# SiLU from ScalarE in every chunk, the second product of the first two chunks as a block, and a new plan of work

## The chip, the cores and the metric

The kernel runs on one core of a Trainium2 chip. The core has a matrix engine (TensorE, "PE" in the profile, with its weight loads as "PEld"), VectorE ("DVE"), ScalarE ("ACT"), GpSimd ("POOL") and SyncE ("SP"), each with a queue of its own that it works through in order. Data are loaded and stored by DMA; a DMA is issued from the queue of an engine. The metric is the time of one execution on the device in microseconds (us). Eleven runs of the kernel before have a median of 275.7 us (272.99 to 277.82).

## The reference

Linear attention, then a SiLU feed-forward layer, over 8 batches of 8 heads, 576 positions and 64 features a head (4608 tokens of 512 features, hidden width 2048):

```python
q_s = exp(q - max(q, -1));  q_s = q_s / (sum(q_s, -1) + 1e-09)      # over features
k_s = exp(k - max(k, 2));   k_s = k_s / (sum(k_s, 2) + 1e-09)       # over positions
kv = einsum('bhsd,bhse->bhde', k_s, v)
x = einsum('bhsd,bhde->bhse', q_s, kv)       # then tokens x (heads * features)
h = x @ w_in                                 # 512 -> 2048
g = h * (1.0 / (1.0 + np.exp(-h)))
out = g @ w_out                              # 2048 -> 512
```

Inputs and output are float32; the kernel multiplies in bf16 and leaves the maxima out, which cancel.

## The kernel before

**Tiling.** The attention works by batch (576 tokens), the feed-forward layer by chunk of 512 tokens, nine of them (chunk 0 takes 576 tokens in its first product, chunk 1 the 448 that are left of 1024). For a batch, `exp` makes eq and ek on ScalarE, two instructions each (`cc` is the half of the heads); `qsum` sums eq on VectorE, `qnorm` divides by the sum, `tr_dma` transposes eq by a DMA into qT; `vcast` writes v in bf16 beside a column of ones into vaug; `kv` multiplies ek by vaug (36 matmuls of 64x65 for each half), so that the last column holds k's sum, and `kvcopy` divides by it. `xt` then makes x transposed in PSUM, `xtcopy` casts it to the tile XT. There is one tile each of eq, ek, vaug and of the loaded q, k and v, so the next batch's exponentials wait until the tile before has been read.

**The first product** is h transposed: W1 is the stationary operand, XT the moving one. In chunks 0 and 1 it is done directly (`mm1`, four matmuls for each 128 hidden features), and `act1` makes SiLU as tanh on ScalarE (tile sg) and `(tanh + 1) * h` on VectorE (line 259); the factor 0.5 comes at the end. From chunk 2 on a part is done by Strassen's scheme in Winograd's form (`product1`, line 316): seven products of half size in place of eight, for a group of 4 x 128 hidden features. The token columns are split in two, the features that are summed over in two, the hidden features in two. XT's sums and differences (`xsum`, tiles XS: S1 to S4) and W1's (`vsum`, tiles TX, once) are the operands; `sum1` (lines 333, 339, 341) combines the seven products in three PSUM banks to four results; `silu1` (line 355) applies ScalarE's SiLU. `std` in a chunk's plan says how many of the four groups are done directly: 2 in chunk 2, 1 in chunks 3 to 8.

**The second product** is direct in chunk 0 (`mm2`, line 476), and by the same scheme in chunks 1 to 8 (`product`, line 411: 14 units of 8 matmuls of 256 columns, seven products in two halves of the tokens). `presum` (lines 369 to 375) makes the sums of GT, the SiLU's output, in two halves of hidden features, into the tiles SW (S1, S2, S4) and in place; `wsum` makes W2's (tiles TW, once); `after` (lines 428 to 447) combines and `qstore` stores from SP. The second product of a chunk runs during the next chunk's first product.

**Order.** Nothing is scheduled by a tool: the order of every engine's queue is the order in which the program writes instructions. `PLAN[t]` gives each piece of work a position within chunk t, counted in units of the first product: `order` is the order of (group, product) pairs, `y` the positions of the 14 (or 16) units of the second product of the chunk before, `ex` of the next batch's four exponentials, `qs`/`qn` of sums and normalisation, `vs`/`ks`/`kc` of casts, kv products and their rescaling, `tp` of the transposing DMA, `ox`/`oc` of the attention product and its casts, `xs`/`xe` of the four XT sums and their engine (0 VectorE, 1 GpSimd), `pa`/`pae` and `pb`/`pbe` of the first and second half of the pre-sums and their engines, `add`, `act`, `ya` of combining steps. `put` gathers the pieces and they are written sorted by position. Chunks 3 to 7 share the plan STEADY. PSUM has eight banks: a ring of six for first products, attention and kv, and two for second products.

**Start.** Batch 0 is loaded from SP in halves. A tiny copy on GpSimd waits for the first half of v, and behind it GpSimd's queue issues the weights (float32 to bf16 on the way) and batch 1's q, k and v: W1 quarter 0, 1, W2 quarter 0, W1 2, W2 1, q, W1 3, k, W2 2, v, W2 3. `heat` keeps TensorE running on a zero tile meanwhile.

Of the kernel before, what the change touches and what calls it, by code (L numbers as in the profile page):

```python
# [15 lines left out]
PLAN = {  # L16
    0: {'y': [5.5, 6.5, 7.5, 8.5, 8.5, 9.5, 10.5, 11.5, 13.5, 13.8, 14.5, 15.5, 15.6, 15.7, 15.9, 22.5], 'ex': [8.9, 10.9, 12.9, 13.4], 'qs': [9.92, 11.4], 'qn': [10.43, 11.41], 'vs': [14.45, 15.05], 'ks': [15.65, 15.75], 'kc': [15.651, 15.751], 'lq': 14.06, 'tp': 12.9, 'ox': [16.35, 16.6], 'oc': [16.36, 18.61], 've': [2, 2]},
    1: {'ex': [0.9, 4.4, 5.9, 5.4], 'qs': [3.9, 4.9], 'qn': [4.91, 5.91], 'vs': [9.3, 10.9], 'ks': [12.4, 13.9], 'kc': [13.41, 14.91], 'lq': 10.45, 'lk': 12.4, 'lv': 15.41, 'tp': 11.4, 'ox': [16.4, 23.6], 'oc': [17.91, 23.61], 've': [1, 1], 'pa': [13.1, 17.7, 18.3], 'pae': [1, 0, 0]},
    2: {'std': 2, 'order': [(3, 1), (2, 1), (2, 6), (3, 6), (2, 2), (2, 7), (3, 2), (3, 7), (3, 5), (2, 5), (2, 4), (3, 3), (3, 4), (2, 3)], 'y': [-2.5, 1.5, 3.5, 4.5, 5.5, 7.5, 9.5, 11.5, 14.0, 15.5, 17.5, 19.0, 20.0, 21.0], 'ex': [-2.6, 0.41, 2.92, 0.43], 'qs': [2.9, 3.9], 'qn': [5.91, 5.91], 'vs': [3.42, 12.4], 'ks': [8.9, 16.4], 'kc': [10.91, 16.41], 'lq': -0.55, 'lk': -2.1, 'lv': 14.41, 'tp': 7.4, 'ox': [18.4, 19.4], 'oc': [18.91, 19.41], 'sl': [0.5, 1.5, 3, 3, 4.5, 8.5, 7, 7], 'add': {(3, 2): 17.02, (2, 7): 13.55, (3, 1): 10.02, (3, 6): 11.55, (2, 5): 17.55, (2, 3): 21.55, (3, 3): 19.55}, 'act': {(2, 6): 13.02, (2, 4): 19.02, (2, 3): 25.02, (2, 5): 17.55, (3, 2): 14.55, (3, 3): 23.02, (2, 1): 11.55, (3, 1): 9.55, (2, 7): 16.02}, 's1': {2: 0, 3: 0}, 'xs': [0.4, 0.9, 7.9, 4.4], 'pa': [16.45, 23.95, 19.45], 'ya': {3: 22.45, 6: 5.5, 5: 15.95, 2: 7.95}, 'm1': [1, 0], 'pb': [-0.4, 0.2, 2.1, 2.2, 2.8], 'xe': [0, 1, 1, 1], 'pae': [1, 1, 1], 'pbe': [0, 0, 0, 0, 0], 've': [1, 2]},
}  # L20
STEADY = {'std': 1, 'order': [(1, 1), (1, 6), (1, 2), (1, 7), (1, 5), (2, 1), (2, 6), (1, 4), (1, 3), (2, 2), (2, 7), (2, 5), (3, 1), (2, 4), (3, 6), (2, 3), (3, 7), (3, 2), (3, 5), (3, 4), (3, 3)], 'y': [1.5, 3.5, 5.5, 7.5, 9.5, 10.0, 15.5, 16.5, 17.5, 18.0, 22.0, 23.5, 24.2, 24.6], 'ex': [-5.1, -0.59, -4.08, -4.57], 'qs': [5.4, 6.4], 'qn': [5.91, 6.41], 'vs': [0.4, 7.42], 'ks': [11.9, 17.4], 'kc': [15.91, 17.41], 'lq': 9.95, 'lk': 16.9, 'lv': 9.41, 'tp': 8.9, 'ox': [22.4, 22.4], 'oc': [22.91, 23.41], 'sl': [2.0, 2.0, 6.5, 4.0], 'add': {(2, 2): 17.02, (1, 2): 6.55, (3, 2): 20.55, (3, 1): 16.55, (3, 7): 21.02, (1, 5): 9.55, (3, 5): 22.55}, 'act': {(1, 5): 12.02, (2, 6): 12.02, (1, 2): 7.02, (3, 1): 19.02, (1, 6): 9.02, (1, 1): 8.02, (3, 3): 25.55, (3, 5): 25.02, (1, 3): 14.02, (2, 2): 15.02, (2, 5): 16.55, (1, 4): 13.02, (3, 7): 23.02, (3, 6): 20.02}, 's1': {1: 1, 2: 0, 3: 0}, 'xs': [-1.6, 0.9, -1.6, 1.4], 'pa': [21.45, 21.95, 23.45], 'pb': [-0.05, 2.46, 2.95, -0.04, 2.95], 'ya': {4: 23.95, 5: 19.45}, 'm1': [0, 0], 'xe': [0, 0, 0, 0], 'pae': [1, 0, 0], 'pbe': [0, 0, 0, 0, 1], 've': [1, 1]}
for _t in range(3, 8):
    PLAN[_t] = STEADY
PLAN[8] = {'std': 1, 'order': [(1, 1), (1, 6), (1, 7), (1, 2), (1, 5), (2, 1), (2, 6), (1, 4), (1, 3), (2, 7), (3, 1), (2, 5), (2, 2), (3, 6), (2, 4), (2, 3), (3, 7), (3, 2), (3, 5), (3, 4), (3, 3)], 'y': [4.5, 5.0, 5.0, 7.5, 9.5, 10.5, 15.5, 17.5, 18.0, 19.0, 22.0, 23.7, 25.5, 26.6], 'sl': [4.0, 10.0, 7.5, 6.0], 'add': {(1, 2): 9.02, (3, 1): 16.02, (1, 5): 9.55}, 'act': {(2, 5): 18.02, (1, 3): 13.02, (1, 4): 15.02, (1, 6): 8.02, (2, 3): 22.02, (3, 3): 25.55, (3, 2): 24.02, (2, 1): 11.02, (3, 5): 22.55, (1, 5): 9.55, (3, 1): 15.55, (1, 2): 8.02, (1, 1): 5.02, (1, 7): 10.02, (2, 4): 19.02, (2, 2): 20.02, (2, 7): 16.02}, 's1': {1: 1, 2: 1, 3: 0}, 'xs': [-11.1, -0.1, 3.4, 7.9], 'pa': [19.95, 20.95, 22.95], 'pb': [-5.55, -4.04, 4.45, -0.04, 2.95], 'ya': {6: 9.5, 3: 27.05, 2: 10.95, 5: 20.95, 1: 7.0, 7: 18.95, 4: 25.7}, 'm1': [0, 0], 'xe': [0, 0, 0, 0], 'pae': [0, 0, 0], 'pbe': [0, 0, 0, 1, 0]}
PLAN[9] = {'y': [0, 1, 2, 3, 4, 5, 6, 7, 8, 9, 10, 11, 12, 13], 'ya': {}, 'm1': [0, 0], 'pb': [-0.5, -0.4, -0.3, 1.9, 2.9], 'pbe': [0, 0, 0, 0, 0]}
TXAT = [(0, (0, 11.76, 1, 0)), (1, (0, 15.77, 1, 0)), (2, (0, 14.78, 1, 1)), (3, (0, 15.79, 1, 1)), (0, (2, 3.1, 0, 0)), (1, (2, 5.6, 0, 0)), (2, (2, 5.6, 0, 0)), (3, (2, 9.6, 0, 1))]
TWAT = [(0, 10.1, 1), (0, 8.7, 1), (0, 13.0, 1), (0, 13.6, 1), (0, 14.7, 0), (0, 19.3, 1), (0, 17.9, 1), (0, 14.0, 1)]

@with_exitstack
def kernel(  # L30
# [26 lines left out]
    part = [[(0, 5 * P), (5 * P, S - 5 * P)]] + [[(0, cut[t + 1] - cut[t])] for t in range(1, NCH)]  # L57
# [34 lines left out]
    def load(b, name, src, ccs=None, eng=nc.sync):  # L92
        if name not in st[b]:
            st[b][name] = ld.tile([128, NG, J * D], FP32, name=name, bufs=LDB[name])
        x = src[b].rearrange("(g r) (p j) d -> g (r p) (j d)", r=2, j=J).rearrange("g x y -> x g y")
        c = slice(0, NG) if ccs is None else slice(2 * ccs, 2 * ccs + 2)
        eng.dma_start(out=st[b][name][:, c, :], in_=x[:, c, :])
# [4 lines left out]
    def exp(b, src, dst, cc):  # L102
        if dst not in st[b]:
            st[b][dst] = ap.tile([128, J, NG * D], BF16, name=dst, bufs=1)
        o = st[b][dst][:, :, cc * 128:(cc + 1) * 128].rearrange("p j (g d) -> p j g d", d=D)
        nc.scalar.activation(out=o, in_=jgd(st[b][src], cc), func=ACT.Exp)  # L106

    def vcast(b, cc, eng):
        o = vaug.rearrange("p j (g e) -> p j g e", e=E1)[:, :, 2 * cc:2 * cc + 2, 0:D]
        if eng is nc.scalar:  # L110
            eng.copy(out=o, in_=jgd(st[b]["vt"], cc))
        else:
            eng.tensor_copy(o, jgd(st[b]["vt"], cc))

    def qsum(b, cc):
# [3 lines left out]
        e = st[b]["eq"][:, :, cc * 128:(cc + 1) * 128].rearrange("p j (g d) -> p j g d", d=D)  # L119
        nc.vector.reduce_sum(out=st[b]["zq"][:, cc], in_=e, axis=AX.X)  # L120
# [15 lines left out]
    def tr_dma(b, eng):  # L136
# [3 lines left out]
        )  # L140

    TG = 6

    def tr(b, g):
        t = ps.tile([128, TG, 128], BF16, name="qtps", tag="ring", bufs=PSB["ring"])
        st[b]["qtps", g] = t
# [541 lines left out]
```

The softmax here doesn't subtract the row's maximum and nothing guards it: scores larger than these inputs give would overflow.

## Time and profile before

The table is from one profiled execution, which took 275.42 us on the device and whose span from the first to the last instruction is 273.6 us.

| | before |
|---|---|
| median of 11 runs | 275.7 us (272.99 to 277.82) |
| profiled execution, its own time | 275.42 us |
| its span | 273.6 us |
| busy: PE / VectorE / ScalarE / GpSimd | 256.9 / 210.6 / 172.7 / 110.9 us |
| mean granted TensorE clock | 0.994 |
| first product of chunk 0 begins | 16.6 us |
| first product of chunk 1 begins | 49.0 us |
| first product of chunk 2 begins | 72.3 us |
| first product of chunk 3 begins | 99.5 us |
| last matmul instructions begin as a block of 128 | 254.8 us |
| ACT_TABLE_LOAD | 12 |

A stage's line in the profile has the stretch (start and end in us from the span's start), its length, and then for PE, PE's weight loads, VectorE, ScalarE and GpSimd the busy time with the number of instructions in brackets, the mean granted TensorE clock, the share of the DMA engines' time that was busy, and GB/s. A line of the timeline has the start, the time, the engine, the source line, the operation, output and inputs, the number of instructions put together, and in square brackets how long the engine had been idle and what ended that. A line of the chain has the start, the time, and the engine with its work. Matmul ends are modelled, so the distance from one matmul to the next says more than the length of one.

### The profile page before, as it was taken

The page shows a single profiled execution, that of the slowest core. Times are in us where ns is not written, and L with a number is a line of the kernel's source. Part 1 is how long each engine was busy: PE and PEld are TensorE (multiplying, and loading weights), DVE is VectorE, ACT ScalarE, POOL GpSimd, SP SyncE. Part 2 cuts the span into 40 slices and gives each one's busy share as a digit, 9 for nine tenths or more (in the row PEclk, how much of TensorE's full clock was granted, in tenths as well). Part 3 has the DMA queues.
Part 4 walks back from the last instruction along what each step waited for, and adds up shares of the span by engine and source line. Part 5 has one row for each costly group of instructions (what it writes and reads, how often), then busy time and mean ns, then how long its engine had stood idle before and what let it go on. Part 6 is the DMA issues. An engine that isn't in the chain of part 4 may idle for free.

```text
span 273.6 us, 6402 instructions
## 1 busy us (share of the span) xinstructions
PE 256.9 (94%) x2594; PEld 191.7 (70%) x2594; DVE 210.6 (77%) x405; ACT 172.7 (63%) x276; POOL 110.9 (41%) x71
## 2 busy tenths in 40 slices
PE   8789989975899999999999999999999999999992
PEld 3356655432467768886888688868886887788882
DVE  2967487498399888889888988888887668877932
ACT  5665576794796499738964896498654457344400
POOL 1561678996159754650644064416332013100000
PEclk9999999999799999999999999999999999999999
DMA  7999999979919850499059805971613012201324
GB/s 257 294 190 244 328 302 215 384 243 217 345 16 366 200 164 20 79 311 363 13 95 361 291 18 99 368 267 30 126 42 78 2 38 58 60 10 32 89 66 115
DMA packets 42925, 46.48 MB, mean 170 GB/s; under 512 B 18576, under 2 KB 30864, under 8 KB 42896
## 3 DMA queue, kind: packets, MB, share of 16 engines
q1 hardware_dynamic: 37856, 38.35, 47.7%
q0 software_dynamic: 5040, 7.73, 12.8%
q8 instruction: 20, 0.33, 0.5%
q14 instruction: 9, 0.07, 0.1%
HBM read 36.70 MB, written 9.44 MB: 169 GB/s over the span
## 4 chain that ended last, share of the span: by engine, by line
PE 69%; DMA 14%; DVE 5%; issue 5%; POOL 4%; ACT 1%; POOLq 0%; ACTq 0%
PE ops L411 34%; PE hps L316 22%; PE hps L233 9%; DMA W<-in_moe_w_out_dram 8%; DMA qT<-eq 3%; DMA qt<-in_q_dram 3%; PE o L203 2%; POOL eq L126 1%; PE kvps L168 1%; DVE TX L291 1%; ACT sg L247 1%; POOL W L516 1%; PE ops L476 1%; DVE zq L120 1%; DVE SW L375 1%
## 5 line engine op out<-in xcount | busy, mean ns | idle before, releaser
L233 PE MATMUL hps<-XT,W 128*128 128x512 bf16 (+3 forms) x320 | 61.3, 337 | 1.9 <-DVE GT L259 1.7
L411 PEld LDWEIGHTS <-GT 128*128 128x128 bf16 x512 | 50.3, 98 | 9.4 <-issue 0.4
L233 PEld LDWEIGHTS <-W 128*128 128x128 bf16 x320 | 31.2, 98 | 25.5 <-issue 3.6
L411 PEld LDWEIGHTS <-SW 128*128 128x128 bf16 x384 | 37.2, 98 | 5.0 <-DVE SW L371 0.2
L355 ACT ACTIVATE GT<-u 128x512 bf16<-128x512 f32 x40 | 24.5, 629 | 24.0 <-DVE u L333 23.8
L126 POOL TENSOR_TENSOR eq<-eq,rzq 128x1152 bf16<-128x1152 bf16 x14 | 29.9, 2154 | 16.7 <-ACT GT L263 9.0
L316 PE MATMUL hps<-XS,TX 128*128 128x256 bf16 x240 | 35.0, 273 | 0.2
L316 PEld LDWEIGHTS <-TX 128*128 128x128 bf16 x320 | 30.6, 98 | 5.6 <-issue 1.6
L411 PE MATMUL ops<-W,GT 128*128 128x256 bf16 x256 | 33.7, 277 | 0.0
L259 DVE SCALAR_TENSOR_TENSOR GT<-sg,hps 128x320 bf16<-128x320 f32 (+3 forms) x64 | 23.5, 414 | 12.8 <-ACT sg L247 12.2
L411 PE MATMUL ops<-TW,SW 128*128 128x256 bf16 x256 | 33.0, 273 | 0.0
L411 PE MATMUL ops<-TW,GT 128*128 128x256 bf16 x256 | 32.9, 273 | 0.0
L333 DVE SCALAR_TENSOR_TENSOR u<-hps,s 128x512 f32<-128x512 f32 x40 | 27.2, 681 | 6.4 <-PE hps L316 4.9
L333 DVE SCALAR_TENSOR_TENSOR u<-hps,u 128x512 f32<-128x512 f32 x40 | 27.4, 686 | 4.0 <-PE hps L316 3.3
L375 POOL TENSOR_TENSOR SW<-GT,SW 128x1024 bf16<-128x1024 bf16 x6 | 13.9, 2321 | 40.1 <-DVE SW L371 35.6
L369 POOL TENSOR_TENSOR SW<-GT 128x1024 bf16<-128x1024 bf16 x7 | 14.9, 2127 | 35.4 <-PE ops L411 35.4
L247 ACT ACTIVATE sg<-hps 128x320 f32<-128x320 f32 (+2 forms) x48 | 21.3, 454 | 9.7 <-DVE GT L259 4.4
L316 PEld LDWEIGHTS <-W 128*128 128x128 bf16 x240 | 23.0, 98 | 3.4 <-issue 0.4
L120 DVE TENSOR_REDUCE zq<-eq 128x18 f32<-128x1152 bf16 x16 | 21.3, 1332 | 3.8 <-ACT eq L106 3.8
L316 PE MATMUL hps<-XT,W 128*128 128x256 bf16 x160 | 24.0, 273 | 0.0
L223 ACT CAST XT<-o 128x512 bf16<-128x512 f32 (+3 forms) x36 | 18.2, 562 | 8.3 <-PE o L203 8.3
L106 ACT ACTIVATE eq<-qt 128x1152 bf16<-128x1152 f32 x16 | 18.5, 1162 | 5.8 <-DMA qt<-in_q_dram 5.7
(77 smaller groups left out, 381.6 us busy)
## 6 DMA issues: line engine op xcount, KB each, us to landing
qt<-in_q_dram SPq DMA_DIRECT2D x6, 1152.0 KB, 8.0
kt<-in_k_dram SPq DMA_DIRECT2D x6, 1152.0 KB, 9.5
vt<-in_v_dram SPq DMA_DIRECT2D x6, 1152.0 KB, 6.5
W<-in_moe_w_in_dram POOLq DMA_DIRECT2D x4, 512.0 KB, 9.9
W<-in_moe_w_out_dram POOLq DMA_DIRECT2D x4, 512.0 KB, 17.7
out_dram<-u SPq DMA_DIRECT2D x16, 128.0 KB, 2.4
out_dram<-u SPq DMA_DIRECT2D x32, 64.0 KB, 2.1
qt<-in_q_dram SPq DMA_DIRECT2D x2, 576.0 KB, 4.1
```

The source lines that it names most:

```text
L106: nc.scalar.activation(out=o, in_=jgd(st[b][src], cc), func=ACT.Exp)
L120: nc.vector.reduce_sum(out=st[b]["zq"][:, cc], in_=e, axis=AX.X)
L126: eng.tensor_tensor(out=e, in0=e, in1=r[:, :, :, None].to_broadcast([128, J, 2, D]), op=ALU.mult)
L223: nc.scalar.copy(out=x, in_=o1[g][:, 0:size])
L233: nc.tensor.matmul(out=hps[:, 0:size], lhsT=W1[:, c, fb * 128:(fb + 1) * 128], rhs=XT[t][:, c, off:off + size], start=(c == 0), stop=(c == ...
L247: nc.scalar.activation(out=sg[:, 0:size], in_=hps[:, 0:size], func=ACT.Tanh, scale=0.5)
L259: nc.vector.scalar_tensor_tensor(out=y, in0=sg[:, h], scalar=1.0, in1=hps[:, h], op0=ALU.add, op1=ALU.mult)
L316: nc.tensor.matmul(out=o[:, f, :], lhsT=l(c, 2 * g + f), rhs=r(c), start=bool(first and f == 0 and c == 0), stop=(c == HK - 1), skip_group ...
L333: nc.vector.scalar_tensor_tensor(out=out, in0=o, scalar=1.0, in1=x, op0=ALU.mult, op1=ALU.add)
L355: nc.scalar.activation(out=y, in_=MP[t, g, x], func=ACT.Silu)
L375: V.tensor_sub(S4[:, f], quad(t, 1, f, 0), S2[:, f])
L411: nc.tensor.matmul(out=o[:, a, :], lhsT=l(f), rhs=r(f), start=bool(first and a == 0 and f == 0), stop=(f == HF - 1), skip_group_check=True,)
```

## The change

- The constant `STD`, below which a chunk's SiLU is made of tanh and a product on VectorE, goes from 2 to 0: ScalarE's Silu function in every chunk. In chunk 0 the units of the second token part cross the border at 512 columns and are written by two instructions (192 and 64 columns).
- Chunk 0's first product runs in units of (128 features, token part) in a given order; its second product (16 units) comes at its end and after it (positions 30.5 to 43.5 of 48), beside batch 1's exponentials. Chunk 1's second product is a block of 14 units behind chunk 1's first product (positions -13 to -1.5 of chunk 2's plan; positions now run through the whole kernel), beside batch 2's exponentials.
- Chunks 3 to 8 do all four groups by the half-size products (`std` 0), chunk 2 two (as before).
- In STEADY three of the four XT sums and six of the eight pre-sums go to GpSimd (before: none and two); one of the two v casts goes from GpSimd to ScalarE; one of the two rescalings of kv (`kvcopy`) goes to ScalarE.
- The start: W1 is loaded in four pieces of 256 and two of 512 columns, all before W2; the first transposes are grouped by head half and their copies divided between VectorE and ScalarE; the second v cast is divided between ScalarE and VectorE; chunk 0's casts and first two units are written half by half.
- The end: the last combining sum and its stores are split by token half; two banks of the ring hold the last products; one of the two last stores is issued by ScalarE.

```diff
-STEADY = {'std': 1, 'order': [(1, 1), (1, 6), (1, 2), (1, 7), (1, 5), (2, 1), (2, 6), ...
+STEADY = {'std': 0, 'order': [(0, 1), (0, 6), (0, 5), (0, 7), (1, 1), (0, 2), (0, 4), ...
...
-'xs': [-1.6, 0.9, -1.6, 1.4], 'xe': [0, 0, 0, 0], 'pae': [1, 0, 0], 'pbe': [0, 0, 0, 0, 1], 've': [1, 1]
+'xs': [-0.204, -0.202, -0.227, 1.9], 'xe': [1, 1, 1, 0], 'pae': [1, 1, 1], 'pbe': [0, 0, 1, 1, 1], 've': [1, 2], 'ke': [0, 1]
...
+WORDER = ['w10', 'w11', 'w13', 'w12', 'w14', 'w15', 'w20', 'q', 'w21', 'k', 'w22', 'v', 'w23']
+STD = 0
+START = {'qn': (0, 0), 'h': [3, 3, 1, 2], 'v': 0, 't': (0, 0, 0, 2), 'x': 1, 'o': 0, 'w': 3}
...
-    def kvcopy(b, cc):
+    def kvcopy(b, cc, act=0):
...
+            if act == 1 or act == 2 and r:
+                nc.scalar.activation(out=y, in_=kp[:, 0:D], func=ACT.Copy, scale=rz[:, 0:1])
+            else:
+                nc.vector.tensor_scalar_mul(out=y, in0=kp[:, 0:D], scalar1=rz[:, 0:1])
...
-    def mm1(t, fb):
-        for off, size in part[t]:
+    def mm1(t, fb, i=0, cs=range(NC)):
+        for off, size in part[t][i:i + 1]:
...
+    def last_add(q, a):
+        o = WP[NCH - 1, "C", a][:, 0:HM]
+        nc.vector.scalar_tensor_tensor(
+            out=q[:, a, :], in0=o, scalar=1.0, in1=q[:, a, :], op0=ALU.mult, op1=ALU.add
+        )
+
+    def last(a):
+        t = NCH - 1
+        q = WP[t, "u2"]
+        last_add(q, a)
+        for half, eng in enumerate((nc.sync, nc.scalar)):
+            b, j = divmod(8 * t + 4 * a + half, J)
+            row = out[b * S:(b + 1) * S, HM:2 * HM].rearrange("(p j) o -> p j o", j=J)
+            eng.dma_start(out=row[:, j, :], in_=q[half * P:(half + 1) * P, a, :])
...
     heat(24)
     for cc in range(2):
         exp(0, "qt", "eq", cc)
         qsum(0, cc)
-        qnorm(0, cc, nc.vector)
+        if cc == 0 or not SB["o"]:
+            qnorm(0, cc, ENG[SB["qn"][cc]])
     exp(0, "kt", "ek", 0)
     vcast(0, 0, nc.scalar)
     exp(0, "kt", "ek", 1)
-    vcast(0, 1, nc.scalar)
...
+    if SB["x"]:
+        xt(0, 0)
+    vcast(0, 1, nc.scalar, (0, 1))
+    vcast(0, 1, ENG[SB["v"]], (1, 2))
+    heat(SB["h"][3])
+    kv(0, 1)
+    if SB["x"]:
+        xtcopy(0, 0, 1)
+    kvcopy(0, 1, 2)
...
+    xt(0, 1)
+    for fb, i in PLAN[0]["order"][:2]:
+        mm1(0, fb, i, range(2))
+    xtcopy(0, 1, 1)
...
-    todo = [[] for _ in range(NCH + 1)]
+    todo = []
+    base = [0]
+    for t in range(NCH):
+        base.append(
+            base[t] + len(PLAN[t]["order"]) + 4 * PLAN[t].get("std", 0) + PLAN[t].get("pad", 0)
+        )

     def put(t, pos, f, *args):
-        todo[t].append((pos, len(todo[t]), f, args))
+        todo.append((base[t] + pos, len(todo), f, args))
```

## The prediction

> **What bounds the kernel now.** I read the page first, then busy time by stage, then the chain of waits, then the timeline of the stages that are not full.
>
> ```profile
> span 273.6 us, 6402 instructions
> PE   8789989975899999999999999999999999999992
> PEclk9999999999799999999999999999999999999999
> ```
>
> The slices show three regions: a start, a thin place in the ninth and tenth slice, and a full TensorE (PE) from the twelfth on. The stages (PE, weight load, VectorE = DVE, ScalarE = ACT, POOL, clock, DMA share, GB/s):
>
> ```profile
> 52.00:62.00 10.00, 7.76 (x40) 3.71 (x38) 7.73 (x13) 9.04 (x14) 9.35 (x6) 1.00 0.85 286
> 62.00:70.00 8.00, 4.04 (x93) 2.11 (x96) 7.17 (x19) 2.94 (x6) 3.87 (x3) 0.96 1.19 219
> 70.00:80.00 10.00, 10.00 (x67) 6.03 (x60) 5.56 (x7) 9.70 (x12) 3.86 (x3) 0.86 0.54 197
> 99.50:126.10 26.60, 26.60 (x302) 21.59 (x300) 22.91 (x43) 20.13 (x32) 11.01 (x6) 1.00 0.53 158
> ```
>
> From 99.5 on PE is busy for all of 26.6 us a chunk, so only less PE work helps there. Between 52 and 70 it idles 6.2 us of 18, and the granted clock dips to 0.86 afterwards. The timeline says why:
>
> ```profile
> 56.95 2.21 ACT L106 ACTIVATE ek<-kt 128x1152 bf16<-128x1152 f32 x2
> 57.18 0.56 DVE L259 SCALAR_TENSOR_TENSOR GT<-sg,hps 128x448 bf16<-128x448 f32 x1
> 57.79 0.92 PE L233 MATMUL hps<-XT,W 128*128 128x448 bf16 x4 [0.62 <-DVE GT L259]
> ```
>
> Two exponentials sit between chunk 1's tanh instructions, the gate product on DVE comes late, and PE waits for a PSUM bank. The chain then waits for batch 2's transposed q:
>
> ```profile
> 61.61 8.02 DMA qT<-eq
> 99.54 1.73 PE hps L233 x8
> 104.74 0.87 PE hps L316 x8
> ```
>
> The last two lines give prices: 0.216 us for a 512-wide matmul, 0.109 for a 256-wide one.
>
> **Steady chunks (3 to 8).** The group done directly (16 matmuls of 512, 3.46 us) becomes seven half-size products (28 of 256, 3.05): 0.41 us less in each of six chunks, -2.4. For it the other engines take, per chunk, against the 26.60 window:
> - DVE: five more combining sums and one more copy of the first product at 0.60 from start to start (110.23, 110.83, 111.42) +3.6; three input sums of 0.33 and four pre-sums of 0.60 leave, two rescalings of 0.2 leave: -3.8. Stays at 22.7.
> - ACT: one v cast +1.1, two rescalings of 64 columns +0.5 (not in the trace on ACT; between 0.20 for one element and 0.38 for 256 columns, I take 0.25): 21.7.
> - POOL: three input sums at 1.15, four pre-sums at 2.13, less one cast: 11.0 + 3.5 + 8.5 - 1.2 = 21.8.
>
> No total passes 26.2, so what decides is the head of a chunk. Counting from the start of the next chunk's first attention product: ACT finishes one SiLU (0.6) and makes four casts at 0.5, done at 2.75. POOL makes S3 from the first two casts, then S1, then S2: done at 2.8 + 2 x 1.1 + 0.1 = 5.1. PE meanwhile runs the attention products (0.7), four first products (0.44 each), two second products (0.87 each), then the new chunk's first product and one more second product (1.3), and asks for S2 at 5.5: 0.4 to spare. The next test is a collision that this trace shows:
>
> ```profile
> 148.31 1.16 POOL L113 CAST vaug<-vt 128x1152 bf16<-128x1152 f32 x1 [0.38 <-DMA vt<-in_v_dram]
> 148.34 1.67 DVE L371 TENSOR_TENSOR SW<-SW,GT 128x1024 bf16<-128x1024 bf16 x1
> ```
>
> A DVE sum of 0.68 that begins inside a POOL instruction ends 0.54 after POOL does. In the new order DVE's second half of S1 meets POOL's S4 (5.1 to 7.2): it ends at 7.75 instead of 7.2, the following two sums at 8.7, the combining sum behind them at 9.4, and PE's fourth-product instruction of group 0 asks for that at 5.5 + 3.9 = 9.4. Nothing is left. I take 0.1 us of wait a head (bounds 0, and 1.0 if one more POOL sum of 2.1 falls in front): six heads, +0.6.
>
> The Trainium skill's "GPSIMD Engine Reference", section 4.1 Engine selection, advises against this move: two-input elementwise work belongs on VectorE, where GpSimd is about 2x slower. The rows are harsher (2.13 against 0.68, 1.15 against 0.42); by that rule alone the moved sums would be a loss, and the steady part would be near zero instead of -1.8. The rows above say that PE does not wait for most of them.
>
> **Chunks 0 and 1.** DVE's gate product disappears (64 instructions, 23.5 us); SiLU replaces tanh. Chunk 0's second half splits at a chunk border into 192 and 64 columns: by the rows of 256 (0.384) and 320 (0.436), an estimate of 0.33 and 0.23, and about 0.8 us for a pair of units with overlap, where PE needs 0.98. Its table load of 1.28 us comes before the first SiLU; six PSUM banks hold 3 us of PE work, so it is hidden.
> - The start: half of the second v cast (1.16 on ACT at 12.97) and the copies of qT are divided between ACT and DVE, and the first W1 piece is half as large. Before, chunk 0's first product ran at 16.6; I take no change (bounds 0.6 to either side, the length of half a cast). It is covered: from 16.6 PE has 15.6 of first products, 10.4 of the first three quarters of the second and 0.5 of kv, so 43.1, and the last W2 quarter comes at 43.75; beyond 0.6 it would show in full.
> - Chunk 0's end: the same bytes are loaded, in 13 transfers and with all of W1 first. The last W2 quarter landed at 43.75 (POOL waited for it until then); four quarter products (3.5) give 47.2; then kv 0.5, reciprocals and rescaling 0.7, attention products and casts 1.2: chunk 1 starts at 49.6 (before 49.0). POOL's queue is empty in front of these issues.
> - Chunk 1: 64 matmuls of 448 columns at 0.189: ends 61.7 (before 66.3, with the waits above). This is the real saving, 4.6 us.
> - Second product of chunk 1 as a block beside batch 2's exponentials: 112 x 0.109 = 12.2, kv 1.0, and about 1.1 of waits (last SiLU, then three pre-sums on DVE): 76.0. What is late next: ACT's last SiLU 62.2, table load 63.5, two q exponentials 65.7, two reductions with reciprocals 67.6, one DVE sum and the normalisation 69.6, transposing DMA 5.3 (4.6 to 8.0 in the trace; it follows batch 3's q on SP) 75.0. On ACT the next batch's q exponential (1.1) waits for that DMA, since the tile is single, and stands ahead of the two rescalings, so the attention product goes at 76.7 and chunk 2 starts at 78.2.
> - Chunk 2: 32 x 0.216 + 56 x 0.109 = 13.0, kv and attention products 1.8: 93.0. ACT has three exponentials and a load first (k lands near 79.7, so 80.0 + 2.2 + 1.3 = 83.5); six banks last until 83.3 and the seventh unit waits 1.2; the second half of kv waits for a SiLU, 0.9, and rescaling on ACT costs 0.6: 95.7. Then three POOL sums with no cover yet, +1.4: 97.1 in place of 99.5, so -2.4. In the kernel before, product and chunk 2 interleaved and lost nothing from 72.3 on; the cover of chunk 2's exponentials is what the block gives away.
>
> Bounds for the front: no waits from chunk 1's end on, 61.7 + 29.0 = 90.7, -8.8; transposing DMA at 8.0 and the POOL sums once more, +1.5.
>
> The kernel changes tables 16 times, not 12:
>
> ```profile
> 75.47 1.28 ACT L263 ACT_TABLE_LOAD   x1
> 76.77 1.08 ACT L263 ACTIVATE GT<-hps 128x512 bf16<-128x512 f32 x2
> ```
>
> The next ACTIVATE starts 0.02 us after the load. The Trainium skill, "ScalarE: Activation LUTs", section What ACT_TABLE_LOAD costs, puts a switch at about 2.66 us with its drain. No drain shows here; by the page the two loads of chunks 1 and 2 that sit on the path would make the sum 2.8 us longer.
>
> **Tail.**
>
> ```profile
> 268.88 0.69 DVE L428 SCALAR_TENSOR_TENSOR u<-ops,u 128x512 f32<-128x512 f32 x1 [1.06 <-PE ops L411]
> 269.60 1.25 SPq L462 DMA_DIRECT2D out_dram<-u  x2
> ```
>
> The last sum is halved (0.69 to about 0.42, between 0.35 for 192 and 0.48 for 320 columns) and its two stores are issued by two queues: -0.3 - 0.6 = -0.9. An issue from ACT is not in the trace; if it costs two of SP's 0.62, -0.3 is left.
>
> **Sum.** -2.4 (front) - 2.4 + 0.6 (steady) - 0.9 (tail) = -5.1 on the profiled execution's 275.42 (span 273.6 and 1.8 around it), which is 0.3 under the median 275.7: **270.3 us**.
>
> **Rivals.**
> 1. The front's waits don't come, because k and the transposed q land early: for it, the median transpose of 5.3 in a stage with fewer loads; against it, ACT's order, which holds whatever the DMAs do. -8 in place of -2.4: 264.7.
> 2. The front gives nothing: the 8.0 us transpose recurs and chunk 2 starts 2.7 later (as at 61.6). 273.0.
> 3. The slower side: POOL's sums at the heads. If S2 and the collided pre-sums come 1.5 us late at every head: 275.4 - 2.4 - 2.4 - 0.9 + 9.0 = 278.7. It decides from 0.95 us a head. For it: no spare at the second test, POOL from 11 to 22 us; against it: DVE's pre-sum of 1.67 at 148.34 left no PE gap.
> 4. SiLU by table does not do what it says in chunk 0, for its three ACT instructions make ACT the bound: without overlap 0.436 + 0.33 + 0.23 = 1.0 against 0.98 of PE, 0.3 us; too small to matter, and counted in the first range.
>
> **Chances.** The forecast 0.48, rival 1 0.18, rival 2 0.16, rival 3 0.18. The likeliest one's own range is 267.5 to 273. With the rivals' sides: 264.5 to 276. What this measurement can tell from no change is about 0.5%, 1.4 us. Faster: 0.46 + 0.18 + 0.11 = 0.75; within: 0.02 + 0.05 + 0.03 = 0.10; slower 0.15.
>
> **What would show it.** Right: chunk 1's 448-wide matmuls without gaps and done by 62; chunk 3's first product near 96 and a short gap before the first S2 product; then heads 26.2 us apart. Wrong: PE waits named POOL XS or DVE SW at each head (rival 3); the transposing DMA the longest wait near 75 (rival 2); chunk 0 slower than 1 us per 128 features, or W1 pieces of 256 columns landing late, which would move everything behind.

## The result and the profile after

| | before | after |
|---|---|---|
| median | 275.33 us (47 runs, 271.38 to 277.82) | 277.89 us (12 runs, 276.44 to 282.04) |
| ratio after/before | | 1.0158, 95% interval 1.0123 to 1.0193 |
| profiled execution, its own time / span | 275.42 / 273.6 us | 278.01 / 276.2 us |
| busy: PE / VectorE / ScalarE / GpSimd | 256.9 / 210.6 / 172.7 / 110.9 us | 257.2 / 199.5 / 186.3 / 162.4 us |

The medians are of all executions and differ by 0.9%; the ratio, here and in the next section, leaves out executions that took over 1.5% longer than the fastest of their kernel. By it the change makes the kernel 1.6% slower; the prediction was 270.3 us, with 264.5 to 276 as its range. From the page of the changed kernel, the span and two rows of the slices:

```profile
span 276.2 us, 6544 instructions
PE   8869999799879969999999999999999999999993
PEclk9999999999998999999999999999999999999999
```

Behind its start, the kernel before had one thin place, slices 9 and 10. Now there are four: slice 3 (the start), slice 8 (chunk 1 begins), slices 11 and 12 (the end of the block) and slice 15 (chunk 3's head). The stages of the changed kernel (stretch, length, then busy time of PE, weight loads, VectorE, ScalarE and GpSimd, the granted clock, DMA share, GB/s), which are chunk 1, the block, chunk 2 and a steady chunk:

```profile
50.00:63.60 13.60, 12.97 (x74) 6.62 (x74) 4.94 (x8) 10.07 (x18) 2.12 (x1) 1.00 0.94 336
63.60:81.80 18.20, 14.82 (x202) 11.70 (x200) 12.59 (x22) 9.92 (x13) 4.34 (x2) 0.99 0.67 196
81.80:98.60 16.80, 16.21 (x169) 9.49 (x167) 13.73 (x23) 14.58 (x25) 8.69 (x5) 0.91 0.73 217
124.10:150.74 26.64, 26.43 (x314) 22.66 (x313) 23.10 (x41) 21.56 (x34) 21.29 (x13) 1.00 0.68 207
```

The block leaves PE idle for 3.4 of 18.2 us. The steady chunk has PE busy for 26.43 of 26.64 us, so it looks as full as before, and it is as long. PE's longest waits up to chunk 3's head, from the view of waits of the changed kernel (waiting engine and line, releaser, us in all, times, longest):

```profile
PE hps L344 <- POOL XS L301: 2.1, 1, 2.1
PE hps L251 <- DMA W<-in_moe_w_in_dram: 2.1, 2, 1.6
PE o L220 <- ACT kvn L196: 1.7, 1, 1.7
PE o L220 <- DMA qT<-eq: 1.3, 1, 1.3
PE ops L445 <- DVE u L467: 1.0, 1, 1.0
```

Where the time went is read best from the attention products (lines 203 and 220), of which each chunk has one pair; a start in us for each kernel:

| | before | after | difference | predicted difference |
|---|---|---|---|---|
| chunk 4's attention products | 121.86 | 124.09 | +2.23 | -2.7 |
| from there to chunk 8's (four steady chunks) | 105.58 | 105.54 | -0.04 | -1.2 |
| from there to the last sum on VectorE | 41.44 | 41.89 | +0.45 | -0.3 |
| from there to the end of the span | 4.77 | 4.71 | -0.06 | -0.9 |

The sum is +2.6, the difference of the spans. No part gave what was expected of it, so there are several causes, and the experiments take them one at a time. Not all went wrong: in the steady chunk the engines' busy times came out as forecast (VectorE 22.7 us forecast and 23.10 measured, ScalarE 21.7 and 21.56, GpSimd 21.8 and 21.29).

### The profile page after: what moved, and what is told of

The parts are those of the page before. It is cut to its first block, busy times and chain, and to the rows that moved or that the text cites. A ratio compares the mean times of both kernels' runs of the same rounds, so it can differ in the third digit from the quotient of the medians.

```text
span 276.2 us, 6544 instructions
## 1 busy us (share of the span) xinstructions
PE 257.2 (93%) x2667; PEld 198.8 (72%) x2667; DVE 199.5 (72%) x332; ACT 186.3 (67%) x315; POOL 162.4 (59%) x102
## 4 chain that ended last, share of the span: by engine, by line
PE 72%; DVE 7%; DMA 7%; POOL 6%; issue 5%; ACT 1%; POOLq 0%; DVEq 0%; ACTq 0%
PE ops L445 29%; PE hps L344 24%; PE hps L251 12%; DMA qT<-eq 4%; PE ops L530 4%; DMA W<-in_moe_w_in_dram 3%; DVE SW L400 3%; DVE u L362 2%; DVE SW L402 1%; PE o L220 1%; PE kvps L178 1%; POOL W L570 1%; POOL XS L299 1%; POOL XS L301 1%; POOL SW L400 1%
## 5 line engine op out<-in xcount | busy, mean ns | idle before, releaser
L445 PEld LDWEIGHTS <-GT 128*128 128x128 bf16 x512 | 49.6, 98 | 7.3 <-DVE u L467 1.3
L362 DVE SCALAR_TENSOR_TENSOR u<-hps,s 128x512 f32<-128x512 f32 x52 | 35.5, 683 | 16.9 <-PE hps L344 16.9
L344 PEld LDWEIGHTS <-TX 128*128 128x128 bf16 x416 | 40.2, 98 | 10.1 <-issue 4.8
L344 PE MATMUL hps<-XS,TX 128*128 128x256 bf16 x312 | 44.7, 273 | 2.8 <-POOL XS L301 2.8
L386 ACT ACTIVATE GT<-u 128x512 bf16<-128x512 f32 x52 | 32.5, 628 | 18.7 <-DVE u L362 18.0
L251 PE MATMUL hps<-XT,W 128*128 128x256 bf16 (+3 forms) x224 | 37.4, 327 | 2.6 <-DMA W<-in_moe_w_in_dram 2.1
L251 PEld LDWEIGHTS <-W 128*128 128x128 bf16 x224 | 22.2, 100 | 17.6 <-issue 3.4
L406 POOL TENSOR_TENSOR SW<-GT,SW 128x1024 bf16<-128x1024 bf16 x11 | 23.5, 2140 | 18.4 <-DVE SW L402 16.8
L281 ACT ACTIVATE GT<-hps 128x192 bf16<-128x192 f32 (+4 forms) x72 | 26.0, 413 | 6.2 <-PE hps L251 4.8
L404 POOL TENSOR_TENSOR GT<-GT 128x1024 bf16<-128x1024 bf16 x12 | 25.5, 2128 | 0.1
L386 ACT ACTIVATE GT<-s 128x512 bf16<-128x512 f32 x26 | 16.3, 627 | 11.7 <-DVE s L362 11.6
L141 POOL TENSOR_TENSOR eq<-eq,rzq 128x1152 bf16<-128x1152 bf16 x9 | 18.9, 2114 | 6.2 <-DVE rzq L134 6.2
```

Source lines behind the costliest of these rows:

```text
L141: eng.tensor_tensor(out=e, in0=e, in1=r[:, :, :, None].to_broadcast([128, n, 2, D]), op=ALU.mult)
L251: nc.tensor.matmul(out=hps[:, 0:size], lhsT=W1[:, c, fb * 128:(fb + 1) * 128], rhs=XT[t][:, c, off:off + size], start=(c == 0), stop=(c == ...
L281: nc.scalar.activation(out=y, in_=hps[:, h], func=ACT.Silu)
L344: nc.tensor.matmul(out=o[:, f, :], lhsT=l(c, 2 * g + f), rhs=r(c), start=bool(first and f == 0 and c == 0), stop=(c == HK - 1), skip_group ...
L362: nc.vector.scalar_tensor_tensor(out=out, in0=o, scalar=1.0, in1=x, op0=ALU.mult, op1=ALU.add)
L386: nc.scalar.activation(out=y, in_=MP[t, g, x], func=ACT.Silu)
```

## The experiments

All are edits of the changed kernel, all compared with the kernel before on the same chip. The marks are the starts of attention products in each one's profiled execution. A mark moves with more than the edit: with the changed kernel's W1 pieces chunk 1's attention products begin anywhere from 49.00 to 50.11 us (e5_tanh aside), and a drop of the granted clock (last section) costs some 1.2 us where it falls. So each edit is also judged by the stretch that it touches.

| run | ratio to before, 95% interval | chunk 4 | chunk 4 to 8 | span |
|---|---|---|---|---|
| (the changed kernel) | 1.0158 (1.0123 to 1.0193) | 124.09 | 105.54 | 276.2 |
| e1_s4_late | 1.0064 (1.0035 to 1.0094) | 123.22 | 103.78 | 273.6 |
| e2_xs3_dve | 1.0130 (1.0066 to 1.0195) | 122.52 | 105.55 | 274.7 |
| e3_w1_quarters | 1.0116 (1.0071 to 1.0161) | 121.61 | 105.53 | 273.7 |
| e4_w_order_before | 1.0415 (1.0370 to 1.0460) | 132.21 | 105.54 | 284.3 |
| e5_tanh | 1.0479 (1.0385 to 1.0574) | 130.74 | 105.53 | 282.9 |
| e6_tail_act | 1.0154 (1.0096 to 1.0212) | 125.77 | 105.50 | 277.8 |
| e9_eq2 | 1.0057 (1.0007 to 1.0108) | 124.20 | 105.54 | 276.3 |
| e8_five | 0.9992 (0.9954 to 1.0029) | 121.71 | 103.78 | 272.1 |
| e11_all | 1.0028 (0.9986 to 1.0070) | 122.89 | 103.81 | 273.1 |
| e12_all_eq2 | 0.9975 (0.9951 to 0.9998) | 120.38 | 103.82 | 270.7 |
| e13_six | 0.9895 (0.9836 to 0.9954) | 118.40 | 103.78 | 268.1 |

**The steady chunks: one sum on GpSimd in the wrong place.** The collision in the changed kernel, from the timelines of GpSimd, VectorE and PE:

```profile
156.08 2.12 POOL L406 TENSOR_TENSOR SW<-GT,SW 128x1024 bf16<-128x1024 bf16 x1
157.41 1.33 DVE L400 TENSOR_TENSOR SW<-GT 128x1024 bf16<-128x1024 bf16 x1
158.85 0.69 DVE L402 TENSOR_TENSOR SW<-SW,GT 128x1024 bf16<-128x1024 bf16 x1
158.79 0.60 PE L445 MATMUL ops<-TW,SW 128*128 128x256 bf16 x4
159.60 0.61 PE L445 MATMUL ops<-TW,SW 128*128 128x256 bf16 x4 [0.21 <-DVE SW L402]
```

GpSimd makes the first half of S4 from 156.08 to 158.20. VectorE's second half of S1 begins inside it and takes 1.33 us instead of 0.68, S2 follows it, and the unit of the second product that reads S2 (line 445) stands still in its middle: its second four matmuls start 0.81 us after the first four, where 0.44 is the rule. The view calls it 0.21, because matmul ends are modelled; from start to start it is 0.37.

```diff
-'pb': [1.45, 1.46, 5.95, 1.46, 1.95]      # steady plan
+'pb': [1.45, 1.46, 5.95, 5.96, 1.95]
```

> The changed kernel with one number of the steady plan changed: the first half of the pre-sum S4 goes behind the last other pre-sum on GpSimd (position 5.96 instead of 1.46). Theory A (the steady chunks gained nothing because VectorE's second half of S1 begins inside GpSimd's S4, takes 1.33 us instead of 0.68, and the product that needs S2 starts 0.37 us late in each of five chunks): the sum takes 0.7 us, the gap goes, the distance from one chunk's attention products to the next falls from 26.64 to about 26.27, and the time from 277.9 to 276.0 (ratio to the kernel before 1.009). Theory B (the sum is slow or TensorE is late for another reason, or S4 at its new place is late for the last product): distance stays at 26.6 or grows, time 277.9 or more.

A chunk takes 26.20 us instead of 26.64, and four of them 103.78 instead of 105.54. The same three steps in this run:

```profile
156.10 0.68 DVE L400 TENSOR_TENSOR SW<-GT 128x1024 bf16<-128x1024 bf16 x1
157.74 2.15 POOL L406 TENSOR_TENSOR SW<-GT,SW 128x1024 bf16<-128x1024 bf16 x1 [2.94 <-PE hps L344]
157.47 1.04 PE L445 MATMUL ops<-TW,SW 128*128 128x256 bf16 x8
```

Theory A held; by the two ratios the gain is 0.9%. The 0.41 us a chunk that the seven products save was there all the time, and the collision took nearly all of it back. The Trainium skill, "SBUF — State Buffer", section Who interferes with whom, describes it as an exclusive lock between VectorE and GpSimd and not a shared rate; the rows agree: the sum ends 0.54 us after GpSimd's instruction, as the one at 148.34 us in the kernel before did, although it began 1.33 us into that instruction and the other 0.03 us. A sum with one operand in PSUM was not held up: inside GpSimd's instruction from 102.86 to 104.99 us of the changed kernel the combining sum at 103.64 (line 362) takes 0.69 us, and the sum of two SBUF operands that follows it at 104.25 (line 400) takes 1.28.

**Chunk 3's head.** In the changed kernel GpSimd still has chunk 2's pre-sums to do when chunk 3's input sums could begin (timeline of GpSimd, and PE's wait that follows):

```profile
97.32 2.12 POOL L402 TENSOR_TENSOR SW<-SW,GT 128x1024 bf16<-128x1024 bf16 x1
99.40 1.16 POOL L303 TENSOR_TENSOR XS<-XT 128x512 bf16<-128x512 bf16 x1
...
101.75 1.15 POOL L301 TENSOR_TENSOR XS<-XS,XT 128x512 bf16<-128x512 bf16 x1
102.95 0.60 PE L344 MATMUL hps<-XS,TX 128*128 128x256 bf16 x4 [2.11 <-POOL XS L301]
```

```diff
+PLAN[3] = dict(STEADY, xe=[0, 0, 0, 0])   # XT's sums of chunk 3 on VectorE
```

> The changed kernel with the first three input sums of chunk 3 (S3, S1, S2) on VectorE instead of GpSimd; all other chunks stay. Theory A (at chunk 3's head TensorE waits 2.1 us because GpSimd is still at the three pre-sums of chunk 2 when the casts of XT are done): the wait named XS at 100.7 us goes, at most 0.3 us of another takes its place, and chunk 4's attention products come 1.8 to 2.1 us earlier (122.1 instead of 124.1); time 276.0. Theory B (GpSimd's pre-sums are late for the product that follows as well): a wait named SW takes the place of the one removed, chunk 4 comes less than 0.5 us earlier, time 277.5 to 277.9.

Both theories missed. The wait only shrinks to 2.01 us, and it is now VectorE that is late. Chunk 4's mark comes 1.57 us earlier, but 1.11 of that are from the start, where chunk 1's attention products begin at 49.00 instead of 50.11. GpSimd, free of the sums, runs S4's first half instead, and VectorE's first input sum falls into it:

```profile
98.43 2.13 POOL L407 TENSOR_TENSOR SW<-GT,SW 128x1024 bf16<-128x1024 bf16 x1
99.72 1.11 DVE L304 TENSOR_TENSOR XS<-XT 128x512 bf16<-128x512 bf16 x1
100.76 0.41 DVE L300 TENSOR_TENSOR XS<-XT 128x512 bf16<-128x512 bf16 x1
```

1.11 us for a sum of 0.41: the same lock. With S4 moved as well (e8_five, below) the sum takes 0.41, the wait 1.32, and chunk 3, counted from its second attention product to chunk 4's first, takes 24.4 us instead of 25.5.

**The start.**

```diff
-WORDER = ['w10', 'w11', 'w13', 'w12', 'w14', 'w15', 'w20', 'q', ...]   # 4 x 256, 2 x 512 columns
+WORDER = ['w10', 'w11', 'w12', 'w13', 'w20', 'q', ...]                 # e3: 4 x 512
+WORDER = ['w10', 'w11', 'w20', 'w12', 'w21', 'q', 'w13', 'k', ...]     # e4: 4 x 512, order of before
```

> The changed kernel with W1 loaded in four pieces of 512 columns instead of four of 256 and two of 512; all of W1 still ahead of W2. Theory A (many small pieces in flight share the transfer rate, so the second and third arrive late): TensorE's waits at 16.5 and 21.1 us for W1 (about 2.1 us in all) shrink to under 0.5 us, chunk 1 starts 1.5 to 2 us earlier (49.5 instead of 51.2), time 276.2. Theory B (the rate is used up by all of W1 being asked for first, whatever the size of the pieces): the waits stay at 1.5 to 2.5 us and the time at 277.9. Theory C (chunk 1's start hangs on the transposing DMA, not on W1): the waits shrink, but chunk 1 starts at 51 us all the same, time 277.9.

> The changed kernel with the weights loaded as in the kernel before: quarters of 512 columns, two of W1, one of W2, one of W1, one of W2, q, the last of W1, k, W2, v, W2; TensorE's order stays that of the changed kernel, with all of the first product first. Theory A of the run with quarters (small pieces are the fault): no wait at 21 us, but a new one of 1 to 3 us near 25 to 29 us for the last quarter of W1, which is asked for seventh; time 277 to 279. Theory B (the order of first product before second product asks for W1 faster than it can come): a wait of 3 us or more for the last quarter, time 279 to 280.

The first product of chunk 0 on PE, in the changed kernel, with quarters, and with the order of before:

```profile
16.54 2.90 PE L251 MATMUL hps<-XT,W 128*128 128x320 bf16 x22 [0.45 <-DMA W<-in_moe_w_in_dram]
21.08 12.48 PE L251 MATMUL hps<-XT,W 128*128 128x320 bf16 x100 [1.65 <-DMA W<-in_moe_w_in_dram]
```

```profile
16.11 15.65 PE L251 MATMUL hps<-XT,W 128*128 128x256 bf16 x124
```

```profile
24.44 1.92 PE L251 MATMUL hps<-XT,W 128*128 128x256 bf16 x16 [1.37 <-DMA W<-in_moe_w_in_dram]
32.37 4.02 PE L251 MATMUL hps<-XT,W 128*128 128x320 bf16 x15 [6.01 <-DMA W<-in_moe_w_in_dram]
```

With quarters the waits are gone, as theory A of e3 said: 2.1 us in the profiled executions, though the changed kernel's was the worst of its kind; its relatives with the same small pieces waited 0.8 to 1.4 us. Chunk 1's first product begins at 49.97 us instead of 51.20. (At chunk 4's mark e3 is 2.5 us ahead, but half of that is a drop of the clock that it does not have.) By the two ratios the gain is 0.4%, with intervals that overlap. With the order of before (theory B of e4) the last quarter is 6.0 us late and the time 285.5 us, more than was expected; from 30.69 to 37.52 us, behind and within this wait, the granted clock is 0.50 as well. So the new order of chunk 0 needs all of W1 ahead of W2, and what was wrong is the size of the pieces, or perhaps the order of two of them, which e3 changes too.

**SiLU or the block?**

```diff
-STD = 0
+STD = 2
```

> The changed kernel with SiLU of chunks 0 and 1 made again of tanh on ScalarE and a product on VectorE (line 259 of the kernel before); the plan stays that of the changed kernel. Theory A (ScalarE's own SiLU is worth something by itself, because the gate product of 0.56 us on VectorE leaves the way from a full to a free PSUM bank): chunk 1's 64 matmuls of 448 columns still take about 12.1 us, since no exponentials lie between, but chunk 0 gets 23 us of VectorE work, half of it in front of the sums of batch 1's q, so that the transposing DMA goes out 2 to 4 us later; less three table loads. Time 279 to 281. Theory B (the gain of chunk 1 came from moving the exponentials out of it, and SiLU brings nothing but table loads): time 277 to 278, with four table loads of 1.28 us less.

Slower than either theory said, 286.8 us. VectorE is busy for 219.1 us instead of 199.5. Chunk 0's first product waits 4.2 us for the gate product, and the block 2.1 us for the last ones of chunk 1, which stand among the pre-sums on VectorE (from the block's first unit to chunk 2's second attention product 20.3 us instead of 16.6; in this stretch the granted clock is also 0.50 for 6.8 us, from 70.98 on, as it is nowhere in the changed kernel's). But chunk 1's own 64 matmuls take 12.26 us, from 55.37 to 67.63, as with SiLU (51.20 to 63.45). In this plan chunk 0 and the block need SiLU, then, though how much of the block's 3.7 us is the gate products and how much the clock is open; chunk 1's shorter product, which the prediction called the real saving, comes from moving the exponentials out.

**The block.** In the changed kernel the chain of work runs from the transposing DMA through ScalarE's exponential and rescalings to chunk 2 (start, length, what):

```profile
72.12 6.43 DMA qT<-eq
...
78.78 0.94 issue
79.72 0.30 ACT kvn L196
```

```diff
-dst, bufs=1)                       # eq and ek
+dst, bufs=2 if dst == "eq" else 1)
-'ex': [-0.707, -5.202, 0.42, 0.294]
+'ex': [-5.201, -5.202, 0.42, 0.294]
```

> The changed kernel with two tiles of eq instead of one, and both q exponentials of batch 3 right behind those of batch 2 in ScalarE's order. Theory A (chunk 2's start and its first SiLU hang on the transposing DMA through ScalarE: the q exponential of batch 3 waits for the DMA until 78.66 us and stands in front of two rescalings; two more exponentials stand in front of the first SiLU at 86.7): the exponentials run at 74 to 76 us, chunk 2's first product begins at 80.7 instead of 81.8, the first SiLU at about 84.5, TensorE's stall for PSUM banks in chunk 2 (1.6 us) goes, and chunk 3 comes 1.5 to 2.2 us earlier; time 276.2. Theory B (batch 3's k, loaded behind the transposing DMA, is what the SiLU then waits for): chunk 2 starts 1 us earlier, but the stall grows by as much; time 277.5 to 277.9.

```profile
79.29 0.57 PE L220 MATMUL o<-qT,kvn 64*64 64x384 bf16 x12 [0.19 <-DMA qT<-eq]
80.68 5.34 PE L251 MATMUL hps<-XT,W 128*128 128x512 bf16 x24
83.16 2.22 ACT L114 ACTIVATE ek<-kt 128x1152 bf16<-128x1152 f32 x2 [1.92 <-DMA kt<-in_k_dram]
87.34 1.89 PE L251 MATMUL hps<-XT,W 128*128 128x512 bf16 x8 [1.32 <-ACT GT L281]
```

The wait of 1.7 us for the rescalings falls to 0.2. Then theory B's k is next (the k exponentials wait for their DMA until 83.16), and 1.3 us of stall stay. From the block's first unit to chunk 3's second attention product it takes 33.1 us instead of 35.1; 1.2 of these 2.0 are a drop of the clock that did not occur here (last section). By the two ratios the gain is 1.0%. The span of this profiled execution does not show it, because the clock fell at two other places (from 51.41 and from 102.61 us).

**The tail.**

```diff
-nc.sync.dma_start(out=row(b)[:, j:j + 5:4, :], in_=q[p])        # product 4 of chunk 8
+nc.scalar.dma_start(out=row(b)[:, j:j + 5:4, :], in_=q[p])
```

> The changed kernel with the two stores of the last chunk's product 4 issued by ScalarE instead of SyncE. Theory A (the halved last sum gained nothing because SyncE issues four stores of 0.62 us one after the other, from 270.5 to 273.4 us, so that the last store goes out as late as before): the last issue is at about 272, and from the last matmul's end to the end of the span 4.1 us instead of 4.7, time 277.3. Theory B (the landing of the stores sets the end whatever the issue, or ScalarE's own issues become the last): 4.7 us as before, time 277.9.

The queues of SyncE in the changed kernel, and of ScalarE in this run:

```profile
270.49 1.25 SPq L516 DMA_DIRECT2D out_dram<-s  x2
271.83 1.55 SPq L505 DMA_DIRECT2D out_dram<-u  x2
```

```profile
272.13 1.40 ACTq L517 DMA_DIRECT2D out_dram<-s  x2
273.63 1.40 ACTq L505 DMA_DIRECT2D out_dram<-u  x2
```

Theory B: moving both stores only moves the queue of four from SyncE to ScalarE; from the last sum to the end it is 4.7 us, as in the changed kernel. One store on each, in e8_five, makes it 4.3.

**Together.**

```diff
+PLAN[3] = dict(STEADY, xe=[0, 0, 0, 0])
-'xe': [1, 1, 1, 0]      # plan of chunk 8
+'xe': [0, 0, 0, 0]
-nc.sync.dma_start(...)  # product 4 of chunk 8
+(nc.scalar if half else nc.sync).dma_start(...)
...
```

> Five edits of the changed kernel together: S4's first half behind the other pre-sums on GpSimd, W1 in quarters, the first three input sums on VectorE in chunk 3 and in chunk 8, and of the two stores of the last chunk's product 4 one on SyncE and one on ScalarE. Theory A (the losses are separate waits on TensorE's path and add up): 277.9 less 2.2 (steady) less 1.2 (start) less 1.9 (chunk 3's head) less 0.8 (chunk 8's head, where TensorE waits 0.85 us for S2) less 0.7 (each queue issues three stores of 0.62 us at the end instead of four and two) = 271.1, ratio to the kernel before 0.99. Theory B (the waits cover each other: what is won early is waited for at the next transposing DMA or GpSimd sum): 274 to 276.

Level with the kernel before, 1.7% under the changed one; its median of 273.65 us lies between the theories, nearer to B. The single gains in the profile add up to the span's (1.2 us at the start, 1.1 in chunk 3, 1.8 in the four steady chunks: 4.1), so these waits are separate ones. But chunk 3's head gave less than the 1.9 us expected, and chunk 8 with the tail got no shorter: VectorE makes the input sums too late there, behind two combining sums, and PE waits 1.3 us for S2 instead of 0.85 (from start to start).

```diff
-PLAN[3] = dict(STEADY, xe=[0, 0, 0, 0])
+PLAN[3] = dict(STEADY, xe=[0, 0, 0, 0], xs=[-1.07, -1.06, -2.0, 1.9])
-'xs': [-0.21, -0.208, -0.207, 4.9]     # chunk 8
+'xs': [-2.05, -2.04, -0.207, 4.9]
-'lk': 20.1, ... 'ex': [-0.707, -5.202, 0.42, 0.294]
+'lk': 19.4, ... 'ex': [-5.201, -5.202, -2.9, -2.901]     # e11, which has two tiles of ek too; e12 as e9
```

> All single cures together: the five edits of the run before (S4's first half late, W1 in quarters, first input sums of chunks 3 and 8 on VectorE, last stores on two queues), with the input sums now placed straight behind the casts of XT, ahead of combining sums that nobody waits for yet; two tiles of eq and of ek, batch 3's k loaded ahead of the transposing DMA instead of behind it, and batch 3's four exponentials ahead of chunk 2's casts. Theory A (each wait found so far is a separate one): the run with five edits had a span of 272.1; less 2 to 2.5 for the exponentials (chunk 2's SiLU no longer waits for them), less 1.2 at chunk 3's head, less 1.1 at chunk 8's: span 267.5, time 269 to 269.5, ratio to the kernel before 0.981. Theory B (k's load beside the transposing DMA slows the DMA, for which TensorE waits before chunk 2): the DMA takes 8 us or more instead of 6.2 and 1 to 2 us of the gain are lost; ratio 0.985 to 0.99.

> As the run with all cures, but with two tiles of eq only; ek single, batch 3's k loaded behind the transposing DMA as in the changed kernel and its k exponentials behind chunk 2's casts. Theory A of the other run (the k exponentials stand in front of chunk 2's first SiLU): 1 to 1.5 us longer than the run with all cures, TensorE's wait for a PSUM bank in chunk 2 1.3 us; ratio 0.985. Theory B (the transposing DMA decides and is quicker here): as short as the other run or shorter.

e11 shows its theory B, and worse; e12, with its span 2.5 us shorter, shows its own theory B, though e11 has a drop of the clock in this place (last section) and e12 has none. The chain in e11 and in e12:

```profile
70.40 8.49 DMA qT<-eq
```

```profile
73.44 6.97 DMA kt<-in_k_dram
80.50 2.22 ACT ek L115 x2
```

With k's load beside it the transposing DMA takes 8.5 us, 2.1 more than in the changed kernel, and PE waits 2.3 us for it. In both runs chunk 3 takes 25.7 us, not 24.4: the input sums had been put ahead of the combining sums, and PE now waits for ScalarE's SiLU (0.75 us) and for a copy (0.2) behind those sums. That placing was a mistake, as the next run shows, where it is undone.

> The cures that held, without those that did not: S4's first half late, W1 in quarters, chunk 3's first input sums on VectorE in their old place in the order, two tiles of eq with batch 3's q exponentials early, the last stores on two queues; chunk 8's input sums stay on GpSimd, and two units of chunk 7's second product go ahead of the product that needs S2, as in the steady plan (positions 0.5 and 1.0 instead of 2.5 and 3.5). Theory A (in the two runs before, the sums of XT in front of VectorE's combining sums cost 1.3 us in chunk 3, since the next SiLU and PSUM banks came late; chunk 8's wait of 0.85 us for S2 is one of order): chunk 3 takes 24.4 instead of 25.7 us, chunk 8's wait falls below 0.2 us, span 268.7, ratio to the kernel before 0.990. Theory B (the combining sums were not the cause): span 270 to 271, ratio 0.9975 as before.

```diff
-'y': [2.5, 3.5, 5.5, ...]     # plan of chunk 8
+'y': [0.5, 1.0, 5.5, ...]
```

Theory A: chunk 3 takes 24.5 us, and with a median of 270.48 us and a ratio of 0.9895 the kernel is 1.0% faster than the kernel before and, by the two ratios, 2.6% faster than the changed one. At chunk 8's head the wait for S2 is gone, though 0.6 us for a pre-sum on GpSimd have come in its place. From the page of this kernel:

```profile
PE   8789999799899989999999999999999999999993
PEclk9999999999999999999999999999999999999999
```

## Why the prediction was wrong

Seven terms of its sum, each with what the profile shows (us):

| term, as predicted | predicted | measured |
|---|---|---|
| chunk 1 begins | 49.6 | 51.20 |
| chunk 1's product | 12.1 | 12.25 |
| product block, to chunk 2's first product | 16.5 | 18.3 |
| chunk 2, to chunk 3's first product | 17.5 | 17.6 |
| POOL sums with no cover at chunk 3's head | 1.4 | 2.1 |
| steady chunk against before | -0.41 + 0.1 | 0.0 |
| tail against before | -0.9 | -0.1 |

- **"The start: I take no change."** This step failed first. It asked whether the cast and the copies on ScalarE were later, and took the smaller first piece of W1 for harmless. The W1 pieces came late, up to 2.1 us, and the text itself said that beyond 0.6 it would show in full. It stood only in the list of what would make the prediction wrong. Quarters removed it: chunk 1 then begins at 49.97 us.
- **Chunk 1.** Length right. But it was booked under SiLU, and e5_tanh shows that the new plan, which moves the exponentials out, made it.
- **"The product block ends 76.0, chunk 2 starts 78.2."** The order of the chain was right, ScalarE's exponential ahead of the rescalings too. It was 3.6 us late: 1.75 came from the steps before, the transposing DMA went out 0.8 later than that, behind GpSimd's and VectorE's normalisations (2.1 us, and 1.6 up to 71.97), and took 6.4 us, not 5.3. A second tile of eq took the exponential off this chain.
- **Chunk 2.** 17.6 against 17.5, but by luck. A drop of the clock that nobody had forecast falls into it (last section); where none falls, in e1_s4_late and e3_w1_quarters, the same stretch takes 16.5. The waits were priced too high: the seventh unit waits 0.3 us there and not 1.2, the second half of kv 0.3 and not 0.9.
- **"POOL's sums, +1.4."** Right mechanism, too small: 2.1. What the step did not see is that VectorE is no refuge while GpSimd works (e2_xs3_dve).
- **"Nothing is left. I take 0.1 us of wait a head."** This is the step that decided the steady chunks. The collision between S4 on GpSimd and S1 on VectorE was found, and priced to 0.55 us; but the test was made on the combining sum behind it, for which group 0's fourth product asks. The wait came earlier, at the unit of the second product that reads S2, where 0.37 us were lost, nearly the whole saving of 0.41. Rival 3 named this mechanism with 1.5 us a head; that its 278.7 us lies near the measured 277.89 is luck, since most of the rest was lost elsewhere.
- **Chunk 8** has a plan of its own, which asks for S2 two units (1.75 us) earlier than the steady plan. The prediction took it for a steady chunk: 0.85 us of wait.
- **"Two stores issued by two queues: -0.6."** The stores of the product before were left out: SyncE issues four in a row, 1.25 us for the first two and 1.55 for the others.
- **The rivals.** Rival 2 (the transposing DMA takes 8 us) and rival 3 both came half true, and their halves add up with the start. Chances were given to mechanisms one at a time; that three small ones come together was given nothing, and it is what happened.

## What to carry to other kernels

A plan that moves elementwise work from VectorE to GpSimd should be tested instruction by instruction for what VectorE does meanwhile: a sum of two SBUF operands that began inside a GpSimd instruction ended 0.27 to 0.54 us after it in the rows above, and the consumer to test is the first one behind the whole chain, whichever engine's product that is. Saved PE time of 0.4 us a stage is worth what the tightest wait in that stage leaves of it. Where a block is given its own place, its DMAs, loads and single buffers are part of the block's length, and the queue of stores at the end counts from the product before the last.

## What had not been expected of the hardware

**The clock falls after a wait.** The changed kernel around chunk 2's start (columns as above; the clock is the third value from the end):

```profile
78.00:80.00 2.00, 0.36 (x6) 0.11 (x4) 0.54 (x1) 1.34 (x3) 0.00 (x0) 1.00 1.02 348
82.00:84.00 2.00, 2.00 (x6) 0.70 (x5) 1.74 (x4) 2.00 (x3) 0.00 (x0) 0.50 1.03 366
86.00:88.00 2.00, 2.00 (x11) 0.92 (x10) 1.98 (x2) 1.99 (x4) 2.00 (x2) 1.00 0.27 78
```

PE waits 1.7 us, and some 1.5 us after it has begun again (80.07) the granted clock falls to 0.50, for 3.41 us (81.54 to 84.95). It is not a matter of course: of nine profiled executions with a wait of 1.4 to 2.3 us at this place, six show the drop; e9_eq2, e12_all_eq2 and e13_six, which wait 0.2 us or less, show none. At chunk 3's head e1_s4_late, e6_tail_act and e9_eq2 have such a drop after the wait of 2.1 us, and the changed kernel has not. It costs 1.2 us where it falls: from the block's first unit to chunk 3's second attention product it takes 33.9 us without it (e1, e3) and 35.1 with it (the changed kernel, e2, e8).

The traces also say when it falls. In each trace with several drops they start a whole number of steps of 3.41 us apart (e6_tail_act: 50.03, 80.75 and 104.64 us, 9 and 7 steps), and each of those ahead of the span's end lasts one step or two. What counts seems to be how long PE is busy within the step just before: at this place 1.12 to 1.72 us of 3.41 in the six executions with a drop (1.70 in the changed kernel, from 78.13 to 81.54), and 1.90 to 2.02 in the three without (e1, e3, e5). A wait that is shorter or divided between two steps cost nothing more. The border is not sharp by this measure: at chunk 3's head of e4_w_order_before PE is busy for 1.54 us of a step, and no drop follows. The Trainium skill, "TensorE: Matmul & The Clock Gate", section What's actually happening, has a clock of half speed after an idle window of about 3.4 us that runs freely; the steps agree with that window, but here one in which PE is busy for half is idle enough. No run moved a wait against the steps on purpose, so that the share decides is read from these executions and not tested.

**Open.** PE's 1.3 us at chunk 3's head and 1.0 us in the block (behind the sums of q on VectorE) are still there in the best version, e13_six; no run tried to remove the second. Why the small W1 pieces come later was not traced to a resource. By their landings, 1024 columns are there at 19.01 us with quarters, at 21.03 in the changed kernel and at 20.00 in e1_s4_late. Small pieces follow each other 1.0 to 1.3 us apart at best and quarters 2.4 to 2.5, so their rate is much the same; the time is lost in single steps (3.6 us ahead of the third piece in the changed kernel, 3.2 ahead of the second in e1), and what holds those up is not known.
